# Operand splits of a gate/up product in pairs of 512 columns, in one fused attention and feed-forward kernel

## The chip, the cores and the metric

The kernel runs on one core of a Trainium2 chip. The metric is the device time of one launch in microseconds. Engine names are those of the profile: PE multiplies matrices (PEld is its weight load), DVE, ACT and POOL are the elementwise engines, SP issues the DMAs. Each takes its instructions in the order in which they were written.

## What is computed

One input x of 2048 rows by 576 columns goes through two branches, and a gate mixes them:

```python
g = sigmoid((x * gate_w).sum(-1, keepdims=True))
a = attention(x)                    # 32 heads of 18, four segments of 512, with a memory
b = (silu(x @ w_gate) * (x @ w_up)) @ w_down          # 576 -> 4608 -> 576
return g * a + (1 - g) * b
```

All of it is fp32. The change touches how the operands of `x @ w_gate` and `x @ w_up` are prepared.

## The kernel before, in words

**Splitting.** PE multiplies in a format that keeps fewer bits than fp32 (`fp32r` here). Each fp32 operand is therefore split in two: a *high* (ACT copies it into the fp32r tile) and a *remainder* (DVE subtracts the high from the source). A product then takes three multiplications: high by high, high by remainder of x, remainder by high of x. So every weight operand passes through ACT and DVE before PE can use it.

**Seven products.** The feed-forward's hidden columns are worked off in 36 slices of 128 (`FT`), for two halves of the rows: 72 *units*, `seq` in the code, numbered 0 to 71 below; half 0 is units 0 to 35. In a unit, gate and up weights form a 2 by 2 arrangement of blocks a11, a12, a21, a22 of 128 x 256 numbers each (x is arranged in the same way), and the four block products per result are made as seven, from sums of blocks. Operand 0 is a11, 1 is a21 + a22, 2 is operand 1 minus a11, 3 is a12, 4 is a11 - a21, 5 is a12 minus operand 2, 6 is a22. POOL makes the four sums. `seven(t, j)` issues the seven matrix instructions of operand j: for each of two blocks high, high, remainder (line 1027), then one for the rest of the rows (line 1030). A unit calls it for j = 0 to 6 in order, with elementwise work on ACT and DVE between: line 1096 after operand 2 (it waits for PE and for the copy of line 1092), 1103 and 1104 after operand 4, 1112 and 1113 after operand 6 (two multiplications on DVE that make the hidden values).

**Ticks.** After each of these pieces the unit calls `tick()`, eight times in all, numbered 0 to 7: tick j follows operand j for j up to 5, tick 6 follows tick 5 at once, tick 7 follows operand 6 and the multiplications. `tick` calls `beat`, which issues first what is *due* at this beat, then down-projection products (line 870) and attention steps. The work for a unit's weights is planned when the unit before it begins: `w_make` returns (number, function) pairs, and number n falls on the n-th beat from there, so 0 to 7 are the ticks of the unit before and 8 to 11 are ticks 0 to 3 of the unit that uses the weights. `HIGH[j]` and `LOW[j]` are the numbers of operand j's high (line 269) and remainder (line 272), `LEAD` places POOL's sums (line 265).

**Buffers.** Operands live in seven places of 2 KB a partition (`wop`); a high of the next unit may be written when the products that read the old one have run. POOL's sums go to three places of 1 KB (`ws`), raw weights to four of 2 KB (`raw`).

**Stages.** Every third unit carries the 16 down-projection groups of the three units before it and is long (about 35 us in the trace); the two others are short (12 to 13 us), with PE going from one operand to the next with at most an attention step between. In half 0 the down weights are split too (line 972, ACT and DVE) and stored; in half 1 they are fetched. The first two units' operands are stored to DRAM in half 0 (`keep`, line 275) and fetched in half 1 (`w_fetch`, line 713) in place of being made, numbers in `FIRST`. At the border of the halves, `x_second` loads, sums and splits the blocks of x for half 1; half of its raw blocks are put in operand places, numbers in `LOADS`, `SUMS`, `PARTS`. Ten further beats (`BREAK`) stand between the halves.

Of the kernel before, what the change touches and what calls it, by code (L numbers as in the profile page):

```python
# [20 lines left out]
P = 128  # L21
# [4 lines left out]
L = 512  # L26
# [17 lines left out]
QUIET = (5, 6, 7)  # L44
HELD = 4
LEAD = 3
HIGH = (2, 3, 3, 7, 7, 8, 9)
LOW = (5, 6, 7, 8, 9, 10, 11)
SHARE = (0, 0, 2, 2, 3, 3, 3, 3)
BREAK = 10  # L50
LOADS = ((-3, 0, 0), (-2, 0, 1), (3, 1, 0), (4, 1, 3), (4, 0, 3), (5, 0, 2), (5, 1, 1), (6, 1, 2))
SUMS = ((2, 0, 1), (9, 0, 4), (10, 1, 1), (11, 1, 4), (12, 1, 2), (13, 1, 6), (14, 0, 2), (19, 0, 6))
PARTS = ((1, 0, 0), (4, 0, 1), (10, 1, 0), (11, 1, 5), (12, 1, 3), (13, 0, 5), (13, 1, 1), (14, 1, 4), (15, 1, 2),
         (17, 0, 2), (17, 1, 6), (18, 0, 3), (20, 0, 4), (22, 0, 6))
FIRST = (9, 10, 11, 15, 17, 17, 19)
SLOT = (0, 3, 2, 1, 4, 6, 5)
RPOS = (0, 1, 4, 2, 5, 6, 3)
BLOCKS = {3: (4, 5), 6: (6, 7), 9: (8, 9), 12: (10, 11), 15: (12,), 18: (13,), 21: (14,), 24: (15,), 27: (16,), 30: (17,)}
# [3 lines left out]
def f32(ap):  # L62
    return ap.bitcast(F32)
# [3 lines left out]
def gated_mix(ctx, tc, xT, xrest, wf, wfr, wfh, wd, wv, wo, beta, cmask, ident, bmask, out):  # L67
# [3 lines left out]
    def pool(st, name, bufs, side="left", space=None):  # L71
        if space is None:
            return st.enter_context(tc.tile_pool(name=name, bufs=bufs, side=side))
        return st.enter_context(tc.tile_pool(name=name, bufs=bufs, space=space))
# [1 line left out]
    dram = pool(ctx, "dram", 1, space=bass.MemoryType.DRAM)  # L76
    stk = dram.tile([2, NSEG, D, 3, L], BF, name="stk")
    vd = dram.tile([NSEG, 2, P, 4, 16, 3, E], BF, name="vd")
    wc = dram.tile([KEPT, 7, P, 4 * P], F32, name="wc")
    rc = dram.tile([FT // 4, 96, 4, 7 * P], F32, name="rc")  # L80
    xrd = dram.tile([7, P, L], F32, name="xrd")
    dc = dram.tile([FT, P, 2 * D], F32, name="dc")
# [134 lines left out]
    def raw_tile():  # L217
        return rp.tile([P, L], F32, name="raw")
# [11 lines left out]

    wraw_of, wops, rhs = {}, {}, []

    def op_tile():
        return wop.tile([P, 2, 2, P], F32R, name="wo_")

    def r_block(h, o):
        i, c = divmod(h, 2)
# [16 lines left out]
    def r_fetch(f):  # L254
        nc.sync.dma_start(f32(rhs[f % 2][:96]).rearrange("p j n -> p (j n)"), rc[f // 4, :, f % 4])

    def w_make(half, f, LOW=LOW):
        g, u = wraw_of.pop(f)
        ops = wops[half, f] = [None] * 7
        a11, a12, a21, a22 = g[:, 0:2], g[:, 2:4], u[:, 0:2], u[:, 2:4]  # L260
        src = [a11, None, None, a12, None, None, a22]

        def total(j, p, q, sub=True):
            src[j] = rp.tile([P, 2, P], F32, name="ws", bufs=3)
            (nc.gpsimd.tensor_sub if sub else nc.gpsimd.tensor_add)(src[j], p(), q())  # L265

        def high(j):
            ops[j] = op_tile()
            nc.scalar.activation(ops[j][:, 0], src[j], AF.Copy)

        def low(j):
            nc.vector.tensor_sub(ops[j][:, 1], src[j], f32(ops[j][:, 0]))  # L272

        def keep(j):
            nc.sync.dma_start(wc[f, j], f32(ops[j]).rearrange("p a k n -> p (a k n)"))

        todo = [(LEAD - 2, lambda: total(1, lambda: a21, lambda: a22, False)),
                (LEAD - 1, lambda: total(2, lambda: src[1], lambda: a11)),
                (LEAD + 2, lambda: total(4, lambda: a11, lambda: a21)),
                (LEAD + 4, lambda: total(5, lambda: a12, lambda: src[2]))]  # L280
        for j in range(7):
            todo += [(HIGH[j], lambda j=j: high(j)), (LOW[j], lambda j=j: low(j))]
            if half == 0 and f < KEPT:
                todo.append((LEAD + j + 3, lambda j=j: keep(j)))
        return sorted(todo, key=lambda t: t[0])


# [1 line left out]
    with ExitStack() as st:  # L289
# [310 lines left out]
        for s in range(NSEG):  # L600
            upd = upd_gen(s - 1) if s else None
            casts = []
            for n, (m, u) in enumerate(chains):
                mid = []
                if s == 0:
                    for z in loads.get(n, []):
                        z()
                    if 0 < n < 6:
                        mid.append(lambda n=n: q_split(*chains[n + 3]))
                    if n in halves:  # L610
                        mid.append(lambda n=n: v_split(*halves[n]))
                if s == 1 and n < 3:
                    cast = masks(*((0, 3), (3, NT), (0, 0))[n])
                    casts.append(cast)
                if s == 1 and 3 <= n < 6:
                    mid.append(casts[n - 3])
                if (s, n) == (1, 7):
                    mid.append(betas)
                if (s, n) == (0, 3):
                    b_load(0)  # L620
                if (s, n) > (0, 3) and blocks:
                    mid.append(lambda z=blocks.pop(0): b_step(*z))
                if 1 <= s < 3:
                    if n == 2:
                        rest_load(2 - s)
                    for j in RSTEP.get(n, ()):
                        mid.append(lambda j=j: rest_split(2 - s, j) if j >= 0 else rest_sum(-j))
                if s == 3:
                    if 2 <= n < 6:
                        first_load(n - 2)  # L630
                    for j, z in FSUM.get(n, []):
                        mid.append(lambda j=j, z=z: first_sum(j, z))
                    for j, z in FSPLIT.get(n, []):
                        mid.append(lambda j=j, z=z: first_split(j, z))
                if s < 3:
                    for kt in ((0, 1), (2, 3), (4,))[n - 6] if s == 0 and n > 5 else (n - 4,) if s and n > 3 else ():
                        raws["x", kt] = x_load(s + 1, kt)
                qk(s, m, u, mid)
                flush(2)
                if upd is not None and n > 0:  # L640
                    next(upd, None)
            if s == 3:
                qst_.close()
                rp = pool(ctx, "rp", 4, side="right")
                wop = pool(ctx, "wop", 7, side="right")
                kq = pool(ast, "kq", 1, side="right")
                for i in range(NST):
                    qst.append(kq.tile([P, 2, L], BF, name=f"qst{i}"))
                    kst.append(kq.tile([P, 2, L], BF, name=f"kst{i}"))
                for i in range(2):  # L650
                    mbs.append(kq.tile([P, 8], F32, name=f"mb{i}"))
                for z in range(2):
                    for j, b, kt in ((0, 2, z), (3, 2, 2 + z), (5, 3, 2 + z)):
                        XO[j][z] = xs_of[b][0][kt]
                wraw_of[0] = [w_load(0, u) for u in range(2)]
                for z in range(2):
                    rhs.append(wop.tile([P, 7, P], F32R, name=f"rh{z}", bufs=1))
                start = w_make(0, 0, LOW[:3] + (7,) + LOW[4:])
            for n in range(8):
                hf, i = divmod(n, 4)  # L660
                flush()
                v_step(s, hf, i)
                if s and n % 2:
                    for bank in range(2):
                        mem_step(s, n // 2, bank)
                if s < 3:
                    if n == 0:
                        xs_of[s + 1] = x_tiles(s + 1)
                    if 1 <= n < 6:
                        x_split(xs_of[s + 1], n - 1, raws["x", n - 1])  # L670
                else:
                    if n == 4:
                        wraw_of[1] = [w_load(1, u) for u in range(2)]
                    if n < 2:
                        first_sum(6, n)
                    elif n < 6:
                        if n < 4:
                            nc.gpsimd.memset(f32(rhs[n - 2][96:]), 0.0)
                        if 3 <= n < 5:
                            r_fetch(n - 3)  # L680
                    if n > 2:
                        for z in stack_loads(0)[2 * n - 6:2 * n - 4]:
                            nc.sync.dma_start(*z)
                    for _ in range((0, 0, 2, 3, 3, 3, 3, 3)[n]):
                        if start[0][0] < 8:
                            start.pop(0)[1]()
# [5 lines left out]
    with ExitStack() as st:  # L692
# [15 lines left out]
        def w_fetch(f):  # L708
            ops = wops[1, f] = [None] * 7

            def one(j):
                ops[j] = op_tile()
                nc.sync.dma_start(f32(ops[j]).rearrange("p a k n -> p (a k n)"), wc[f, j])

            return [(j + 2 if f else FIRST[j], lambda j=j: one(j)) for j in range(7)]

        kp = pool(ast, "kp", 2, side="right")
        ap = pool(ast, "ap", 2, side="right")
# [273 lines left out]
            return [(f // CH, i, hf, hs, ds, yas[half], half) for i in range(8) for hf in range(2)]  # L992

        def x_second(new, rest):
            r = {}
            todo = []

            def load(z, q):
                b, kt = ((0, z), (1, z), (0, 2 + z), (1, 2 + z))[q]
                r[z, q] = wop.tile([P, L], F32, name="wo_") if z else raw_tile()[:, :L]  # L1000
                nc.sync.dma_start(r[z, q], xT[HALF[1][b], :, kt])

            def total(z, j):
# [224 lines left out]
```

## Time and profile before

| what | value |
|---|---|
| median of 3 runs | 1721.14 us (1719.92 to 1722.72) |
| the profiled execution | 1722.04 us, span of its instructions 1720.3 us |
| before the units, units of half 0, units of half 1, end | 221.57, 722.76, 683.67, 92.00 us |
| DMA | 328.05 MB, mean 191 GB/s |
| granted clock of PE | 1.00 |

How to read the rows of the next section: a row of the timeline has the start and the length in us, the engine, the line of the kernel, the operation, what it writes and reads, the shape and how many were merged; brackets tell how long the engine was idle before it and what it waited for. A row of busy time in stretches has the window, its length, then for each engine the busy time with the number of instructions in brackets, the granted clock, the DMAs' busy share and GB/s. A row of grouped instructions has count, then busy us and mean ns, then the idle time before them. Tiles named `wo__` with a number are operand places, each made by one call.

### The profile page before, as it was taken

How to read it: one execution, taken by the hardware profiler on the slowest of the kernel's cores; microseconds unless marked ns; L12 is line 12 of the kernel's file. 1: busy time of each engine (PE TensorE's matmuls, PEld its weight loads, DVE VectorE, ACT ScalarE, POOL GpSimd, SP SyncE). 2: the span in 40 equal slices, each digit the busy share in tenths (PEclk: the TensorE clock that was granted, in tenths of full speed). 3: DMA queues.
4: the chain of work that ended last, by engine and by line, in shares of the span. 5: the costliest groups of instructions: out<-in, count | busy, mean ns of one | idle time of the engine just before them, and what ended most of it. 6: DMA issues, size and time to landing. Idle time of an engine off the chain costs nothing.

```text
span 1720.3 us, 34819 instructions
## 1 busy us (share of the span) xinstructions
PE 1705.2 (99%) x11868; PEld 1479.8 (86%) x11868; DVE 1362.3 (79%) x3231; ACT 1084.6 (63%) x2123; POOL 937.9 (55%) x1194
## 2 busy tenths in 40 slices
PE   9999999999999999999999999999999999999999
PEld 7899978888888888888888788888888888888899
DVE  6557588888888889888889777787787788788655
ACT  7666576775776677567666756665666576566411
POOL 4434546666665655656566555565555555555311
PEclk9999999999999999999999999999999999999999
DMA  8654499998998898997979986787778677767633
GB/s 282 235 186 140 162 310 186 224 228 178 218 230 197 180 216 203 183 209 195 201 159 256 289 172 145 178 183 162 151 180 188 142 164 181 170 131 167 191 120 136
DMA packets 524002, 328.05 MB, mean 191 GB/s; under 512 B 411184, under 2 KB 460336, under 8 KB 523824
## 3 DMA queue, kind: packets, MB, share of 16 engines
q1 hardware_dynamic: 523824, 325.83, 78.0%
q8 instruction: 93, 1.52, 0.4%
q14 instruction: 85, 0.70, 0.1%
HBM read 165.76 MB, written 76.09 MB: 141 GB/s over the span
## 4 chain that ended last, share of the span: by engine, by line
PE 84%; DVE 7%; ACT 3%; issue 2%; DMA 2%; POOL 1%; SPq 0%; DVEq 0%; ACTq 0%; POOLq 0%
PE bank L1027 33%; PE bank L870 26%; PE bank L160 10%; PE bank L1030 5%; PE bank L728 4%; PE bank L776 2%; PE bank L777 1%; PE bank L415 1%; DVE hl L972 1%; DVE scr L734 1%; PE bank L461 1%; DVE dw L972 1%; DVE p L760 1%; PE bank L351 1%; DVE xo L138 1%
## 5 line engine op out<-in xcount | busy, mean ns | idle before, releaser
L761 POOL TENSOR_TENSOR p<-pe,p 128x512 f16<-128x512 f32 x320 | 378.4, 1182 | 417.0 <-DVE p L760 399.9
L870 PE MATMUL bank<-dw,hh 128*128 128x320 f32 (+1 forms) x2304 | 487.1, 304 | 1.5 <-DVE ya L880 1.5
L870 PEld LDWEIGHTS bank<-dw,hh 128*128 128x128 f32 x2304 | 381.1, 189 | 13.9 <-DVE ya L880 3.3
L746 ACT ACTIVATE pe<-bank,mb 128x512 f32<-128x512 f32 (+3 forms) x512 | 247.9, 526 | 196.2 <-DVE mb L734 183.1
L870 PE MATMUL bank<-dw,hl 128*128 128x320 f32 (+1 forms) x1152 | 340.6, 296 | 1.4 <-DVE hl L138 1.4
L734 DVE CUSTOM_DVE_ANT_0 scr<-bank,cm 128x512 bf16<-128x512 f32 (+3 forms) x512 | 246.5, 481 | 6.8 <-PE bank L728 0.2
L880 DVE TENSOR_TENSOR ya<-bank,ya 128x320 f32<-128x320 f32 x352 | 158.2, 453 | 77.8 <-PE bank L870 77.0
L870 PEld LDWEIGHTS bank<-dw,hl 128*128 128x128 f32 x1152 | 217.9, 189 | 1.9 <-DVE hl L138 1.9
L1030 PE MATMUL bank<-xr,rh 128*128 128x512 f32 x504 | 196.3, 390 | 0.0
L754 POOL TENSOR_SCALAR_AFFINE_SELECT pe<-pe 128x256 f32<-128x256 f32 (+1 forms) x320 | 151.6, 474 | 52.1 <-ACT pe L746 42.6
L760 DVE CAST p<-pe 128x512 f16<-128x512 f32 x320 | 160.6, 502 | 0.0
L265 POOL TENSOR_TENSOR ws<-raw 128x256 f32<-128x256 f32 x140 | 116.3, 831 | 16.1 <-DMA raw<-in_wf_dram 8.4
L728 PE MATMUL bank<-kst,qst 108*128 108x512 bf16 (+3 forms) x512 | 124.6, 305 | 0.3 <-DMA kst<-stk 0.2
L972 DVE TENSOR_TENSOR hl<-row,hh 128x512 fp32r<-128x512 f32 x120 | 108.4, 903 | 8.9 <-ACT hh L971 8.5
L1030 PEld LDWEIGHTS bank<-xr,rh 128*128 128x128 f32 x504 | 94.6, 188 | 20.4
L1104 DVE TENSOR_TENSOR row<-bank,row 128x512 f32<-128x512 f32 x72 | 49.7, 690 | 62.6 <-ACT bank L1103 62.5
L746 ACT ACT_TABLE_LOAD x69 | 88.5, 1283 | 10.8 <-DVE mb L734 9.8
L1089 ACT ACTIVATE bank<-bank 128x512 f32<-128x512 f32 x72 | 41.9, 582 | 79.8 <-PE bank L1030 76.7
L1106 ACT ACT_TABLE_LOAD x71 | 91.1, 1283 | 1.3
L1099 ACT ACTIVATE row<-bank 128x512 f32<-128x512 f32 x72 | 43.2, 600 | 71.5 <-PE bank L1030 71.3
L265 POOL TENSOR_TENSOR ws<-raw,ws 128x256 f32<-128x256 f32 x70 | 58.8, 840 | 49.9 <-DVE wo__22504 L272 9.7
L1103 ACT ACTIVATE bank<-bank 128x512 f32<-128x512 f32 x72 | 42.2, 587 | 65.5 <-PE bank L1030 65.1
(2170 smaller groups left out, 4123.1 us busy)
## 6 DMA issues: line engine op xcount, KB each, us to landing
raw<-in_wf_dram SPq DMA_DIRECT2D x140, 256.0 KB
rh<-rc SPq DMA_DIRECT2D x72, 336.0 KB
dc<-dw SPq DMA_DIRECT2D x36, 576.0 KB
dw<-dc SPq DMA_DIRECT2D x36, 576.0 KB
stk<-q SPq DMA_DIRECT2D x32, 384.0 KB
draw<-in_wd_dram SPq DMA_DIRECT2D x36, 288.0 KB
rc<-rt SPq DMA_DIRECT2D x42, 224.0 KB
vd<-vps SPq DMA_DIRECT2D x8, 912.0 KB
```

What stands on the lines that cost most here:

```text
L160: nc.tensor.matmul(t, st[n], mv[n], start=(n == 0), stop=(n == 13))
L265: (nc.gpsimd.tensor_sub if sub else nc.gpsimd.tensor_add)(src[j], p(), q())
L728: nc.tensor.matmul(t[:, c:c + w], qs[:KR, pr, P * i:P * i + P], ks[:KR, pr, 0:w], start=True, stop=True)
L734: nc.vector.tensor_tensor_reduce(scr[:, :w], t[:, c:c + w], cm[:, L - w:L], -SCALE, 3.0e38, OP.add, OP.min, m[:, k:k + 1])
L746: nc.scalar.activation(pe[:, c:c + w], t[:, c:c + w], AF.Exp, bias=m[:, k:k + 1], scale=SCALE)
L754: nc.gpsimd.affine_select(d, d, pattern=pat, compare_op=OP.is_ge, fill=0.0, base=0, channel_multiplier=1)
L760: nc.vector.tensor_copy(p[:, 0], pe)
L761: nc.gpsimd.tensor_sub(p[:, 1], pe, p[:, 0])
L870: nc.tensor.matmul(ts[m], p, q[:, cs], start=(n == 0), stop=(n == 3 * CH - 1))
L880: nc.vector.tensor_add(ya[:, i, cs], t, ya[:, i, cs])
L1027: nc.tensor.matmul(t, w[:, p, z], x[z][:, q], start=first and n == 0, stop=False, skip_group_check=True)
L1030: nc.tensor.matmul(t, rem[:, RPOS[j]], XR[j], start=False, stop=True, skip_group_check=True)
```

## The change

Operands are made in pairs, `PAIRS = ((0, 3), (1, 2), (4, 6), (5,))`. A pair shares one place of 4 KB (operand 5 keeps one of 2 KB), one high of 512 columns on ACT and one remainder of 512 columns on DVE; so a unit has four highs and four remainders in place of seven and seven. To make that possible the sources lie side by side: operands 0 and 3 are the raw gate block, 1 and 2 are two halves of one `ws` place of 2 KB, and operand 4's sum is written over a21, so that 4 and 6 are the raw up block; operand 5's sum has a place of its own (`wt`). Each place exists once. The numbers are rewritten: pair by pair, highs on 4, 3, 8, 9 and remainders on 6, 7, 10, 11. Stores and fetches of kept operands move a whole place at a time, and the raw x blocks that lay in operand places lie in `ws`, in operand 5's place and in the place of operands 4 and 6, with other numbers in `LOADS`.

```diff
-HIGH = (2, 3, 3, 7, 7, 8, 9)
-LOW = (5, 6, 7, 8, 9, 10, 11)
+PAIRS = ((0, 3), (1, 2), (4, 6), (5,))
+HIGH = (4, 3, 8, 9)
+LOW = (6, 7, 10, 11)
-LOADS = ((-3, 0, 0), (-2, 0, 1), (3, 1, 0), (4, 1, 3), (4, 0, 3), (5, 0, 2), (5, 1, 1), (6, 1, 2))
+LOADS = ((-3, 0, 0), (-2, 0, 1), (2, 1, 0), (4, 0, 3), (5, 0, 2), (6, 1, 1), (8, 1, 3), (8, 1, 2))
-FIRST = (9, 10, 11, 15, 17, 17, 19)
+FIRST = ((9, 10, 18, 15), (4, 3, 8, 6))
...
-    def op_tile():
-        return wop.tile([P, 2, 2, P], F32R, name="wo_")
+    def op_tile(g, shape=None, dtype=F32R):
+        n = len(PAIRS[g])
+        return wop.tile(shape or [P, 2, n, 2, P], dtype, name=f"wo{'abcd'[g]}_", bufs=1)
+
+    def op_home(f, g):
+        return wc[f, :, 8 * P * g:8 * P * g + 4 * P * len(PAIRS[g])]
+
+    def op_views(ops, g, t):
+        for i, j in enumerate(PAIRS[g]):
+            ops[j] = t[:, :, i]
...
-        src = [a11, None, None, a12, None, None, a22]
+        part = {4: a21}
+        src = {0: g, 2: u}
+        tile_of = {}
         def total(j, p, q, sub=True):
-            src[j] = rp.tile([P, 2, P], F32, name="ws", bufs=3)
-            (nc.gpsimd.tensor_sub if sub else nc.gpsimd.tensor_add)(src[j], p(), q())
+            if j == 1:
+                src[1] = rp.tile([P, 4, P], F32, name="ws", bufs=1)
+                part[1], part[2] = src[1][:, 0:2], src[1][:, 2:4]
+            elif j == 5:
+                part[5] = src[3] = rp.tile([P, 2, P], F32, name="wt", bufs=1)
+            (nc.gpsimd.tensor_sub if sub else nc.gpsimd.tensor_add)(part[j], p(), q())
-        def high(j):
-            ops[j] = op_tile()
-            nc.scalar.activation(ops[j][:, 0], src[j], AF.Copy)
-        def low(j):
-            nc.vector.tensor_sub(ops[j][:, 1], src[j], f32(ops[j][:, 0]))
+        def high(n):
+            tile_of[n] = op_tile(n)
+            op_views(ops, n, tile_of[n])
+            nc.scalar.activation(halves(n, 0), flat(n), AF.Copy)
+        def low(n):
+            nc.vector.tensor_sub(halves(n, 1), flat(n), f32(halves(n, 0)))
...
-        for j in range(7):
-            todo += [(HIGH[j], lambda j=j: high(j)), (LOW[j], lambda j=j: low(j))]
+        for n in range(4):
+            todo += [(HIGH[n], lambda n=n: high(n)), (LOW[n], lambda n=n: low(n))]
             if half == 0 and f < KEPT:
-                todo.append((LEAD + j + 3, lambda j=j: keep(j)))
+                todo.append((LOW[n] + 1, lambda n=n: keep(n)))
...
-                start = w_make(0, 0, LOW[:3] + (7,) + LOW[4:])
+                start = w_make(0, 0)
...
-            return [(j + 2 if f else FIRST[j], lambda j=j: one(j)) for j in range(7)]
+            return [(FIRST[f][n], lambda n=n: one(n)) for n in range(4)]
...
-                r[z, q] = wop.tile([P, L], F32, name="wo_") if z else raw_tile()[:, :L]
+                if not z:
+                    r[z, q] = raw_tile()
+                elif q == 0:
+                    r[z, q] = rp.tile([P, L], F32, name="ws", bufs=1)
+                elif q == 1:
+                    r[z, q] = op_tile(3, [P, L], F32)
+                else:
+                    if not pair:
+                        pair.append(op_tile(2, [P, 2, L], F32))
+                    r[z, q] = pair[0][:, q - 2]
```

More of the change, by code (lines that the diff above doesn't have):

```diff
@@ L78, in gated_mix @@
     vd = dram.tile([NSEG, 2, P, 4, 16, 3, E], BF, name="vd")
-    wc = dram.tile([KEPT, 7, P, 4 * P], F32, name="wc")
+    wc = dram.tile([KEPT, P, 28 * P], F32, name="wc")
     rc = dram.tile([FT // 4, 96, 4, 7 * P], F32, name="rc")
@@ L231, in gated_mix, with op_flat @@
     wraw_of, wops, rhs = {}, {}, []
-    def op_tile():
-        return wop.tile([P, 2, 2, P], F32R, name="wo_")
+    def op_tile(g, shape=None, dtype=F32R):
+        n = len(PAIRS[g])
+        return wop.tile(shape or [P, 2, n, 2, P], dtype, name=f"wo{'abcd'[g]}_", bufs=1)
+    def op_flat(t):
+        return f32(t).rearrange("p a j k n -> p (a j k n)")
+    def op_home(f, g):
[3 more added lines that the diff above has]
+            ops[j] = t[:, :, i]
     def r_block(h, o):
@@ L255, in r_fetch, with w_make @@
         nc.sync.dma_start(f32(rhs[f % 2][:96]).rearrange("p j n -> p (j n)"), rc[f // 4, :, f % 4])
-    def w_make(half, f, LOW=LOW):
+    def w_make(half, f):
         g, u = wraw_of.pop(f)
@@ L271, in low @@
-        def low(j):
-            nc.vector.tensor_sub(ops[j][:, 1], src[j], f32(ops[j][:, 0]))
-        def keep(j):
-            nc.sync.dma_start(wc[f, j], f32(ops[j]).rearrange("p a k n -> p (a k n)"))
+            if j == 1:
[4 more added lines that the diff above has]
+            (nc.gpsimd.tensor_sub if sub else nc.gpsimd.tensor_add)(part[j], p(), q())
@@ new lines, in flat, with halves, keep @@
+        def flat(n):
+            return src[n].rearrange("p k n -> p (k n)")
+        def halves(n, z):
+            return tile_of[n][:, z].rearrange("p j k n -> p (j k n)")
+        def high(n):
[4 more added lines that the diff above has]
+            nc.vector.tensor_sub(halves(n, 1), flat(n), f32(halves(n, 0)))
+        def keep(n):
+            nc.sync.dma_start(op_home(f, n), op_flat(tile_of[n]))
@@ L277, in w_make @@
         todo = [(LEAD - 2, lambda: total(1, lambda: a21, lambda: a22, False)),
-                (LEAD - 1, lambda: total(2, lambda: src[1], lambda: a11)),
+                (LEAD - 1, lambda: total(2, lambda: part[1], lambda: a11)),
                 (LEAD + 2, lambda: total(4, lambda: a11, lambda: a21)),
-                (LEAD + 4, lambda: total(5, lambda: a12, lambda: src[2]))]
-        for j in range(7):
-            todo += [(HIGH[j], lambda j=j: high(j)), (LOW[j], lambda j=j: low(j))]
+                (LEAD + 4, lambda: total(5, lambda: a12, lambda: part[2]))]
@@ L644, in gated_mix @@
                 rp = pool(ctx, "rp", 4, side="right")
-                wop = pool(ctx, "wop", 7, side="right")
+                wop = pool(ctx, "wop", 1, side="right")
                 kq = pool(ast, "kq", 1, side="right")
@@ L709, in w_fetch, with one @@
             ops = wops[1, f] = [None] * 7
-            def one(j):
-                ops[j] = op_tile()
-                nc.sync.dma_start(f32(ops[j]).rearrange("p a k n -> p (a k n)"), wc[f, j])
-            return [(j + 2 if f else FIRST[j], lambda j=j: one(j)) for j in range(7)]
+            def one(n):
+                t = op_tile(n)
+                op_views(ops, n, t)
+                nc.sync.dma_start(op_flat(t), op_home(f, n))
+            return [(FIRST[f][n], lambda n=n: one(n)) for n in range(4)]
         kp = pool(ast, "kp", 2, side="right")
@@ L994, in x_second @@
         def x_second(new, rest):
-            r = {}
+            r, pair = {}, []
             todo = []
```

## The prediction, made before the result

> **What bounds the kernel now.** I read the page first, then the busy time in stretches, then the waits, then the timeline of single units. On the page:
>
> ```profile
> span 1720.3 us, 34819 instructions
> PE 1705.2 (99%) x11868; PEld 1479.8 (86%) x11868; DVE 1362.3 (79%) x3231; ACT 1084.6 (63%) x2123; POOL 937.9 (55%) x1194
> PE 84%; DVE 7%; ACT 3%; issue 2%; DMA 2%; POOL 1%; SPq 0%; DVEq 0%; ACTq 0%; POOLq 0%
> PE bank L1027 33%; PE bank L870 26%; PE bank L160 10%; PE bank L1030 5%; PE bank L728 4%; PE bank L776 2%; PE bank L777 1%; PE bank L415 1%; DVE hl L972 1%; DVE scr L734 1%; PE bank L461 1%; DVE dw L972 1%; DVE p L760 1%; PE bank L351 1%; DVE xo L138 1%
> ```
>
> PE is busy 99% and carries 84% of the chain that ended last; the products of this change's operands (L1027) are a third of it. The span is 1720.3 us; that execution took 1722.04 us, 0.9 above the median of 1721.14, and my sum is added to the median. Cut by stage (before the units, units of half 0, units of half 1, the end), columns PE, PEld, DVE, ACT, POOL:
>
> ```profile
> 221.57:944.33 722.76, 715.72 (x5094) 610.26 (x5092) 634.36 (x1504) 491.34 (x950) 443.64 (x580) 1.00 0.92 210
> 944.33:1628.00 683.67, 682.77 (x4830) 588.23 (x4829) 537.88 (x1311) 435.73 (x843) 371.17 (x471) 1.00 0.76 174
> ```
>
> In the 72 units PE is idle 722.76 - 715.72 = 7.0 us in half 0 and 0.9 us in half 1, at a granted clock of 1.00. So whatever is taken off another engine can return about 8 us here, no more. The reader should keep this asymmetry: little to win, and any new wait of PE costs its full length. DVE is the second engine (634 of 723 us in half 0), and works in order.
>
> **What the change removes.** The highs (L269, ACT) and remainders (L272, DVE) of the operands, over both halves:
>
> ```profile
> 214.00:944.00 730.00, 146.10 (x252) 1.00 0.92 210
> 944.00:1628.00 684.00, 135.96 (x238) 1.00 0.76 174
> 214.00:944.00 730.00, 98.95 (x252) 1.00 0.92 210
> 944.00:1628.00 684.00, 92.58 (x238) 1.00 0.76 174
> L971 ACT ACTIVATE hh<-row 128x512 fp32r<-128x512 f32 x120 | 75.3, 628 | 0.9 <-DVE row L1113 0.9
> L972 DVE TENSOR_TENSOR hl<-row,hh 128x512 fp32r<-128x512 f32 x120 | 108.4, 903 | 8.9 <-ACT hh L971 8.5
> L138 DVE TENSOR_TENSOR hl<-row,hh 128x512 fp32r<-128x512 f32 x24 | 17.8, 743 | 11.3 <-ACT hh L137 11.0
> ```
>
> The first two rows are L272 (DVE), the next two L269 (ACT), 490 = 70 units x 7 each. A remainder costs (146.10 + 135.96) / 490 = 0.58 us on average, a high 191.5 / 490 = 0.39. Three remainders of 512 columns at 0.74 to 0.90 and one of 256 at 0.58 are 2.8 to 3.3 us, against 4.0 for seven: DVE is relieved by 0.7 to 1.2 us a unit. Three highs at 0.63 and one at 0.39 are 2.3, against 2.7: ACT by 0.4. All of this lies beside PE.
>
> [...]
>
> **What the change moves.** This decides. The operands of a unit are read one after the other, 7 products each; highs are read by products 1, 2, 4, 5, remainders from the third on. A pair is written whole, so it can only be written after both old operands are read, and must be there before the earlier of the two is read. With the tick numbers of HIGH and LOW (8 ticks a unit, number 8 is the next unit's tick 0):
>
> - Operand 0's remainder moves from tick 5 to 6, where operand 1's was; the unit reads it first.
> - Operand 1's moves from tick 6 to 7, where operand 2's was: behind the two multiplications L1112 and L1113, the first of which waits for the last operand of the old unit. It is read second.
> - Operand 4's moves from tick 1 to 2, behind L1096. Operand 5's moves from tick 2 to 3, where operand 6's was.
>
> So each new deadline can be tested in the old trace: put the remainder that stood at the later place beside the products that will now need it. Operand 1, in a unit without down-products:
>
> ```profile
> 1264.20 1.00 DVE L272 TENSOR_TENSOR wo__17859<-raw,wo__17859 128x256 fp32r<-128x256 f32 x1
> 1265.13 0.51 DVE L272 TENSOR_TENSOR wo__17872<-ws,wo__17872 128x256 fp32r<-128x256 f32 x1
> 1265.22 1.52 PE L1027 MATMUL bank<-xo,wo__17859 128*128 128x512 f32 x6
> 1265.56 0.68 DVE L1112 TENSOR_TENSOR row<-bank,row 128x512 f32<-128x512 f32 x1
> 1266.16 0.68 DVE L1113 TENSOR_TENSOR row<-row 128x512 f32<-128x512 f32 x1
> 1266.76 0.95 DVE L272 TENSOR_TENSOR wo__17874<-ws,wo__17874 128x256 fp32r<-128x256 f32 x1
> 1266.80 1.52 PE L1027 MATMUL bank<-xo,wo__17872 128*128 128x512 f32 x6
> ```
>
> Seven products take 1266.80 - 1265.22 = 1.58 us, 0.226 each, so the third product of operand 1 starts at 1266.80 + 0.45 = 1267.25. The remainder at the later place ends at 1266.76 + 0.95 = 1267.71: 0.46 us too late, and it will be twice as wide. The same for operand 0 (first three rows) and operand 5 (last three):
>
> ```profile
> 499.96 1.72 DVE L972 TENSOR_TENSOR dw<-draw,dw 128x576 fp32r<-128x576 f32 x1
> 500.52 1.52 PE L1027 MATMUL bank<-xo,wo__6605 128*128 128x512 f32 x6
> 501.60 0.62 DVE L272 TENSOR_TENSOR wo__6635<-ws,wo__6635 128x256 fp32r<-128x256 f32 x1
> ...
> 976.02 0.41 DVE L272 TENSOR_TENSOR wo__13668<-ws,wo__13668 128x256 fp32r<-128x256 f32 x1
> 978.28 1.64 PE L1027 MATMUL bank<-xo,wo__13668 128*128 128x512 f32 x6
> 978.64 0.80 DVE L272 TENSOR_TENSOR wo__13702<-raw,wo__13702 128x256 fp32r<-128x256 f32 x1
> ```
>
> Operand 0 is needed at 500.97, the later place ends at 502.22: 1.25 late, because DVE still splits a down weight. Operand 5 is needed at 978.73, the later place ends at 979.44: about 0.6 to 0.7 late. I took this difference for all 70 units (first and last of them here):
>
> ```profile
> 221.57 1.62 PE L1027 MATMUL bank<-xo,wo__2469 128*128 128x512 f32 x6
> 221.71 0.42 DVE L272 TENSOR_TENSOR wo__2471<-ws,wo__2471 128x256 fp32r<-128x256 f32 x1
> ...
> 1617.64 1.66 PE L1027 MATMUL bank<-xo,wo__22833 128*128 128x512 f32 x6
> 1618.96 0.45 DVE L272 TENSOR_TENSOR wo__22835<-ws,wo__22835 128x256 fp32r<-128x256 f32 x1
> ```
>
> The later place ends after the need in 18 units for operand 0, 20 for operand 1, 1 for operand 4 and 16 for operand 5; 39 units have at least one. A stall of PE also delays the reads behind it, so a unit counts its largest shortfall only: the sum is **25.5 us**, 18.9 of it in half 0.
>
> Two things shift that sum. The wider remainder ends later by 256 columns, 0.69 - 0.42 = 0.27 us alone (L1112 and wo__2471 bracket it); with 0.27 on every unit the sum is 37. Against it DVE has fewer operations ahead, which helps only where it was behind and not where it waited for PE (L1112 and L1096 do, in most short units); 0.27 earlier in every unit gives 16, 0.5 earlier 10. I take them as cancelling, since about half the late units wait at L1112 or L1096 just before. The waits that exist today can shrink:
>
> ```profile
> PEld bank L1027 <- ACT bank L1103: 6.3, 10, 1.3
> PEld bank L1027 <- DVE bank L1096: 5.0, 9, 1.1
> ```
>
> I take off 2 us of these 11, as ACT's and DVE's order around L1103 and L1096 hardly changes.
>
> **The other edits.** Stores of kept operands (units 0 and 1 alone) become four of up to 512 KB. Today's:
>
> ```profile
> 227.75 5.12 DMA wc<-wo__2473
> 232.96 0.42 ACT L269 ACTIVATE wo__2722<-ws 128x256 fp32r<-128x256 f32 x1 [2.25 <-DMA wc<-wo__2473]
> ```
>
> 256 KB took 5.12 us and held ACT 2.25 us, three ticks behind. Twice the bytes at the same distance holds ACT longer, at most by another 5 us a store; PE sees part. I take 2 us, from 0 to 10, for both units. At the border of the halves the raw x blocks are loaded into the new homes up to four ticks later, and the third fetch comes at tick 0 of the unit that reads it at its fifth operand, some 7 us later, against 5.12 for half the bytes in the row above. I take 1 us, from -1 to 5. Fewer DMA issues on SP cost nothing: PE waits for none of them. The sums on POOL stay at four of the same size, and their waits for a free buffer get shorter, off the chain.
>
> Sum: 25.5 - 2 + 2 + 1 = 26.5, so 1721.1 + 26.5 = **1748 us**.
>
> **The rivals.**
>
> 1. *Relief before deadline (faster).* DVE's 0.7 to 1.2 us a unit come in ahead of the late places. For: in half 0 DVE is 88% busy, and where it runs behind PE everything later moves forward. If it gains more than the shortfall in nearly all units (the largest is 1.7), no new wait stays and at most 8 us of today's idle goes: about 1714. The point is a relief of about 1 us before tick 6; against it, two of the three remainders removed (operands 3 and 4, ticks 0 and 1) lie behind these ticks, and L1112 waits for PE whatever DVE has saved. [...]
> 2. *New waits and relief meet* within 3 us of now: 1721. It needs 1 us of relief at the late places, which leaves under 4 us of shortfall.
> 3. *Wider remainders meet POOL.* The late places already show 0.80 and 0.95 where 0.41 is the time alone; if the wide ones take 0.9 to 1.2 there, shortfalls grow by about 0.45 without relief: 47 us, 1768. [...]
> 4. *The edit does less than it says*: the shortfalls are absorbed, and only the two stores and the border count: about 1726.
>
> **How the numbers follow.** Forecast 0.66; rivals 0.12, 0.05, 0.10 and 0.07 in order. A measurement here tells about 0.2% (3.4 us) from nothing. Faster 0.12 is rival 1; within 0.2% is 0.05; slower is 0.66 + 0.10 + 0.07 = 0.83. The range runs from 1722, which leaves out rival 1 and half of rival 2, to 1768: the forecast's own terms span 10 to 47 us, and rival 4 lies inside.
>
> **What would show it.** PE idle in front of L1027, released by DVE L272, in units without down-products, at the third product of the first, second and sixth operands, 20 to 45 us in all, more in half 0. Today's sum of such waits is one row under L272 (us, times):
>
> ```profile
>   PEld bank L1027: 1.9, 6
> ```
>
> DVE's busy time for L272 down by 50 to 80 us, ACT's for L269 by about 30, with PE's idle up all the same. The forecast is wrong if L272 releases PE for under 10 us, if the lost time lies at the border of the halves, or if L1096 or L1103 become the releasers.

## The result and the profile after

The changed kernel takes **1761.19 us** (median of 5 runs, 1760.46 to 1762.06) against 1721.14: a ratio of 1.0229, 95% interval [1.0218, 1.0241]. That is 40 us more. The profiled execution took 1762.06 us with a span of 1760.0. The forecast was 1748 us, with a range from 1722 to 1768.

In the new kernel lines have moved: the high is L294 (L269 before), the remainder L297 (L272), POOL's sums L283, a unit's products L1062 and L1065, and L1092, L1096, L1103, L1106, L1112 and L1113 are now L1127, L1131, L1138, L1141, L1147 and L1148. The page:

```profile
span 1760.0 us, 34418 instructions
PE 1720.0 (98%) x11868; PEld 1473.7 (84%) x11868; DVE 1310.4 (74%) x3021; ACT 1064.1 (60%) x1913; POOL 939.2 (53%) x1194
PE 63%; ACT 7%; DVE 6%; issue 5%; POOL 3%; DMA 2%; SPq 1%; DVEq 0%; ACTq 0%; POOLq 0%
```

DVE has 51.9 us less to do and ACT 20.5, and the kernel is slower. PE's share of the chain fell from 84% to 63%, but the shares add up to 87% of the span here and to 99% before, so the chain alone doesn't tell how much PE lost. The stages, cut where the units begin, change halves and end:

```profile
222.71:966.72 744.01, 723.74 (x5094) 607.42 (x5092) 607.30 (x1396) 480.21 (x843) 444.04 (x579) 1.00 0.89 204
966.72:1669.60 702.88, 690.11 (x4830) 585.34 (x4829) 514.58 (x1209) 426.18 (x741) 373.52 (x474) 1.00 0.73 170
```

Half 0 is 21.3 us longer and half 1 19.2, at the same clock and with the same number of PE instructions. PE's idle time went from 7.0 to 20.3 us and from 0.9 to 12.8. Its *busy* time also rose, by 8.0 and 7.3 us: where products follow one another, only 0.23 us of each counts; the last one ahead of a wait counts with its full 0.39 (the two products ahead of the wait shown below count 0.61). So idle time alone shows too little of a wait. Who waits for the remainders (us, times; the PE row was missing before, the PEld row stood at 1.9, 6):

```profile
  PEld bank L1062: 55.6, 85
  PE bank L1062: 24.2, 42
  POOL ws L283: 5.2, 4
  POOL wt L283: 2.6, 2
```

One such wait, in a short unit of half 1, at operand 1:

```profile
1292.67 0.58 ACT L1138 ACTIVATE bank<-bank 128x512 f32<-128x512 f32 x1 [0.53 <-PE bank L1065]
1293.16 0.62 ACT L294 ACTIVATE woa__17301<-raw 128x512 fp32r<-128x512 f32 x1
1293.69 0.68 ACT L772 ACTIVATE pe<-bank,mb 128x512 f32<-128x512 f32 x1
1294.39 1.28 ACT L1141 ACT_TABLE_LOAD   x1
1294.39 1.17 POOL L787 TENSOR_TENSOR p<-pe,p 128x512 f16<-128x512 f32 x1 [4.62 <-DVE p L786]
1294.84 1.27 DVE L297 TENSOR_TENSOR woa__17301<-raw,woa__17301 128x512 fp32r<-128x512 f32 x1
...
1295.68 0.63 ACT L1141 ACTIVATE row<-row 128x512 f32<-128x512 f32 x1
...
1296.23 0.74 POOL L283 TENSOR_TENSOR raw<-raw 128x256 f32<-128x256 f32 x1
1296.35 0.69 DVE L1147 TENSOR_TENSOR row<-bank,row 128x512 f32<-128x512 f32 x1 [0.24 <-ACT row L1141]
1296.93 0.73 POOL L283 TENSOR_TENSOR wt<-raw,ws 128x256 f32<-128x256 f32 x1
1296.95 1.26 DVE L1148 TENSOR_TENSOR row<-row 128x512 f32<-128x512 f32 x1
1297.45 0.61 PE L1062 MATMUL bank<-xo,wob__17289 128*128 128x512 f32 x2
1298.14 0.68 DVE L297 TENSOR_TENSOR wob__17289<-ws,wob__17289 128x512 fp32r<-128x512 f32 x1
1298.87 1.20 PE L1062 MATMUL bank<-xo,wob__17289 128*128 128x512 f32 x4 [0.81 <-DVE wob__17289 L297]
```

Operand 1's third product is due at 1297.45 + 0.45 = 1297.90. Its remainder (`wob__17289`, last but one row) stands behind the two multiplications, as the prediction put it, ends at 1298.82, and PE goes on at 1298.87, 0.97 us late. Two more things can be read here. The first multiplication (L1147) waits for ACT: the wide high L294 at tick 4 stands between ACT's copy L1138 and its activation L1141. And two of DVE's operations are longer where POOL works: the wide remainder takes 1.27 us beside POOL's and 0.68 beside none, and the second multiplication 1.26 beside POOL's, against 0.68 on average in the 35 units in which POOL does nothing beside it.

To put a price on each place, I set the start of every operand's first and third product beside the same product of the kernel before. The difference is the lag; what it grows by between two such points is lost between them. At third products: operand 0 lost 6.8 us, operand 1 15.3, operand 5 11.0, in 45 units. Another 8.6 us appear at the first products of operands 1, 2 and 6, most of it as 0.11 or so behind each wait: the product behind one that waited starts 0.34 us after it instead of 0.23, so a wait costs more than its length here. The old waits at operand 4 shrink by 2.8 in half 0, and 1.1 is lost ahead of the first unit. Followed back on DVE, the last wait ahead of a late remainder is at L1147 for 25 of the 27 of operand 1 (19 times for ACT's L1141) and at L1131 for 16 of the 17 of operand 5: the instructions behind which the new numbers put them.

### The profile page after: what moved, and what is told of

Same layout as the page of the kernel before. It is cut to its first block, busy times and chain, and to the rows that moved or that the text cites. A ratio compares the mean times of both kernels' runs of the same rounds, so it can differ in the third digit from the quotient of the medians.

```text
span 1760.0 us, 34418 instructions
## 1 busy us (share of the span) xinstructions
PE 1720.0 (98%) x11868; PEld 1473.7 (84%) x11868; DVE 1310.4 (74%) x3021; ACT 1064.1 (60%) x1913; POOL 939.2 (53%) x1194
## 4 chain that ended last, share of the span: by engine, by line
PE 63%; ACT 7%; DVE 6%; issue 5%; POOL 3%; DMA 2%; SPq 1%; DVEq 0%; ACTq 0%; POOLq 0%
PE bank L896 24%; PE bank L1062 24%; PE bank L1065 4%; PE bank L161 3%; PE bank L754 3%; PE bank L802 2%; ACT L1141 1%; PE bank L803 1%; ACT pe L772 1%; POOL ws L283 1%; ACT bank L1138 1%; ACT row L1141 1%; POOL p L787 1%; DVE p L786 1%; DVE hl L998 1%
## 5 line engine op out<-in xcount | busy, mean ns | idle before, releaser
L1065 PE MATMUL bank<-xr,rh 128*128 128x512 f32 x504 | 196.6, 390 | 0.0
L786 DVE CAST p<-pe 128x512 f16<-128x512 f32 x320 | 156.6, 491 | 0.0
L1065 PEld LDWEIGHTS bank<-xr,rh 128*128 128x128 f32 x504 | 94.6, 188 | 20.8
L1139 DVE TENSOR_TENSOR row<-bank,row 128x512 f32<-128x512 f32 x72 | 49.7, 690 | 63.3 <-ACT bank L1138 63.0
L1138 ACT ACTIVATE bank<-bank 128x512 f32<-128x512 f32 x72 | 42.1, 584 | 71.6 <-PE bank L1065 71.5
L1131 DVE TENSOR_TENSOR bank<-bank,row 128x512 f32<-128x512 f32 x72 | 50.3, 699 | 46.2 <-PE bank L1065 25.3
L1147 DVE TENSOR_TENSOR row<-bank,row 128x512 f32<-128x512 f32 x72 | 49.8, 691 | 46.3 <-PE bank L1065 27.0
```

Of the source, the lines that this page charges most:

```text
L786: nc.vector.tensor_copy(p[:, 0], pe)
L1065: nc.tensor.matmul(t, rem[:, RPOS[j]], XR[j], start=False, stop=True, skip_group_check=True)
```

## The experiments

**The theory** was that the places (tick numbers) of the remainders make the loss, and that DVE's relief buys nothing. **The rivals**: the wide operation (its length, POOL beside it, both operands of a pair at once); ACT's order; stores, fetches and the border. The kernel before took 1720.5 to 1721.7 us beside these runs (medians); differences under about 3.4 us, the prediction's measure, are not told from nothing by the times alone. Where operands are named with a number of us, it is the loss at their third products.

**1. All remainders one tick earlier.**

```diff
-LOW = (6, 7, 10, 11)
+LOW = (5, 6, 9, 10)
```

> The changed kernel with its four remainders one tick earlier (numbers 5, 6, 9, 10 for 6, 7, 10, 11); pairs, places and widths stay. Theory 'place': PE waits because the tick puts the remainder behind work that itself waits for PE (L1112 and L1113 above all), so nearly all of the 33 us gained at the third products of operands 0, 1 and 5 goes: 1718 to 1730 us. Rival 'width': an operation of 512 columns is what is late, as it collides with POOL and runs 0.7 to 0.9 us wherever it stands: over 1745. Rival 'homes': stores, fetches and raw x blocks in new homes carry the loss: 1755 to 1761.

Measured: 1728.94 us (1727.84 to 1730.62), ratio 1.0053 [1.0038, 1.0068]. The waits are gone (rows as above):

```profile
  PEld bank L1062: 2.6, 7
  POOL wt L283: 1.6, 1
  PE bank L1062: 0.2, 1
```

32 of the 40 us go with the place alone; pairs, width, stores and border are all still there, and hold at most 8.

**2. The kernel before, with the late numbers.** Seven highs and seven remainders of 256 columns, moved to where the change has them.

```diff
-HIGH = (2, 3, 3, 7, 7, 8, 9)
-LOW = (5, 6, 7, 8, 9, 10, 11)
+HIGH = (4, 3, 3, 4, 8, 9, 8)
+LOW = (6, 7, 7, 6, 10, 11, 10)
```

> The kernel before, seven single highs and remainders in seven places of 2 KB, with only their numbers set to those of the changed kernel (highs 4, 3, 3, 4, 8, 9, 8; remainders 6, 7, 7, 6, 10, 11, 10). 'Place': it loses what the changed kernel lost or more, since DVE has three more operations to do at the same places: 1755 to 1775 us. 'Width' and 'homes': no change from before, 1719 to 1727.

Measured: 1751.83 us (1751.38 to 1752.38), ratio 1.0186 [1.0171, 1.0201], a little under what was expected. The late places, of highs and remainders together, cost 31 us without any pair. Rows of those who wait for L272:

```profile
  POOL ws L265: 179.8, 82
  PEld bank L1027: 45.6, 67
  PE bank L1027: 21.0, 33
  POOL pe L754: 1.0, 3
```

Operands 0, 1 and 5 lose 3.8, 5.2 and 18.7 us. POOL waits 179.8 us for its `ws` places; of the waits that the late remainders stand behind on DVE, none was ended by POOL. ACT's order is in these 31 us too, since the highs of operands 0 and 3 also moved, from ticks 2 and 7 to tick 4: ahead of the first multiplication DVE waits 19.1 us for ACT's L1106, where it waited 3.6 before.

```profile
L1112 DVE TENSOR_TENSOR row<-bank,row 128x512 f32<-128x512 f32 x72 | 49.6, 690 | 36.7 <-ACT row L1106 19.1 <-PE bank L1030 15.0 <-ACT dw L971 1.8
```

**3 to 6. One or two remainders one tick earlier.** The changed kernel, with the first, second, sixth, or first and second number of `LOW` put back by one:

```diff
-LOW = (6, 7, 10, 11)
+LOW = (6, 6, 10, 11)    # operands 1 and 2
+LOW = (6, 7, 10, 10)    # operand 5
+LOW = (5, 7, 10, 11)    # operands 0 and 3
+LOW = (5, 6, 10, 11)    # operands 0 to 3
```

Operands 1 and 2:

> The changed kernel with the remainder of operands 1 and 2 alone one tick earlier (6 for 7), ahead of the two multiplications. 'Place': the third products of operand 1, where 15.3 us were gained on the trace before, no longer wait, with about 3 us that follow each wait: 1761 - 18 = 1743, 1738 to 1750. 'Width' or 'homes': 1757 to 1763.

Operand 5:

> The changed kernel with the remainder of operand 5 alone one tick earlier (10 for 11); this one is 256 columns wide as before. 'Place': the third products of operand 5, where 11.0 us were gained, no longer wait, with some 2 us that follow: 1761 - 13 = 1748, 1744 to 1754. 'Width': operation of 256 columns, so what it costs now is not width; if width elsewhere is the cause, its shift changes nothing, 1757 to 1763.

Operands 0 and 3:

> The changed kernel with one number of LOW moved, 6 to 5: the remainder of operands 0 and 3 is issued one tick earlier, everything else stays. In the changed kernel PE loses 6.8 us at the third product of operand 0 and 15.3 us at that of operand 1. If the waits at the deadlines were independent of one another, the 6.8 us and the 1 us or so of refilling behind them would go: 1753 us. If a wait taken away comes back at the next deadline (as it did where operand 5's remainder alone was moved), operand 1's third product, which follows 1.6 us later with the same DVE queue before it, takes up most of it: over 20 us there, and 1756 to 1761 us.

Operands 0 to 3:

> The changed kernel with two numbers of LOW moved, 6 to 5 and 7 to 6: the remainders of operands 0 and 3 and of operands 1 and 2 one tick earlier, those of 4, 6 and 5 as in the changed kernel. Independent waits: the 6.8 and 15.3 us at the first two operands go, with some 3 us of refilling, the 11 us at operand 5 stay: 1735 to 1737 us. If the waits move on to the next deadline, operand 5's third product rises above 14 us and the time is 1739 to 1743 us. In either case the kernel with all remainders one tick earlier, 1729 us, tells what operand 5 alone is worth when the others are in time: 7 us by the first, 10 to 14 by the second, where it was worth 3 when the others were late.

| remainders moved | op. 0 | op. 1 | op. 5 | us (lowest to highest) | ratio and interval |
|---|---|---|---|---|---|
| none (the change) | 6.8 | 15.3 | 11.0 | 1761.19 (1760.46 to 1762.06) | 1.0229 [1.0218, 1.0241] |
| 0 and 3 | 0 | 19.8 | 10.7 | 1759.58 (1756.66 to 1760.46) | 1.0215 [1.0197, 1.0234] |
| 5 | 12.0 | 17.8 | 0 | 1758.13 (1756.97 to 1758.33) | 1.0221 [1.0206, 1.0236] |
| 1 and 2 | 6.9 | 0 | 12.0 | 1742.56 (1742.41 to 1745.54) | 1.0137 [1.0121, 1.0154] |
| 0 to 3 | 0 | 0.3 | 11.7 | 1737.24 (1735.00 to 1739.37) | 1.0091 [1.0073, 1.0109] |

The expectation for operands 1 and 2 held. That for operand 5 failed: the time lies in the range that was given to 'width', but the waits at operand 5 did go and came back elsewhere, which neither reading said. Of the two readings given for the others, the moving wait held for operands 0 and 3, and 0 to 3 together came closest to independence. Operand 1 is worth its price (18.6 us); operands 0 and 5 return 1.6 and 3.1, neither clear of the noise and not the 7 to 12 that PE loses at them. Their waits go, but reappear at the deadlines behind: for operand 5 moved, those who wait for L297 are

```profile
  PEld bank L1062: 47.6, 65
  PE bank L1062: 24.0, 39
```

so PE's own idle for remainders is as before (24.2), on fewer operands. I read it so, and no run tests it alone: a wait of PE lets DVE catch up, and without it DVE meets the next deadline further behind. With operands 0 to 3 in time, operand 5's step is worth 1737.24 - 1728.94 = 8.3 us (with operands 4 and 6, which move too). So a place has no fixed price: operand 5's tick is worth at most some 3 us or about 8, depending on the others.

**7. Pair highs, seven remainders of 256 columns** on the numbers of before:

```diff
+LOWS = (5, 6, 7, 8, 9, 10, 11)
-            todo += [(HIGH[n], lambda n=n: high(n)), (LOW[n], lambda n=n: low(n))]
+            todo += [(HIGH[n], lambda n=n: high(n))]
+            for i, j in enumerate(PAIRS[n]):
+                todo += [(LOWS[j], lambda n=n, i=i: low(n, i))]
```

> The changed kernel with its four highs and places, but seven remainders of 256 columns at the numbers of the kernel before (5, 6, 7, 8, 9, 10, 11). 'Place': the waits for remainders go whatever the highs and homes are: 1722 to 1730 us, about where the kernel with four remainders one tick earlier landed (1728.9). If it lands under that by over 3 us, the width of the remainders cost something there; if above by over 3, their number did. 'Homes': 1752 or more.

Measured: 1727.24 us (1725.34 to 1729.19), ratio 1.0036 [1.0022, 1.0049], as 'place' expected. The four wide remainders of run 1, on time, are no better than seven narrow ones: fewer, wider operations gain PE nothing here.

**8. Highs earlier too**, on top of run 1.

```diff
-HIGH = (4, 3, 8, 9)
+HIGH = (4, 3, 7, 8)
-LOW = (6, 7, 10, 11)
+LOW = (5, 6, 9, 10)
```

> The changed kernel with remainders at 5, 6, 9, 10 and the last two highs one tick earlier too (4, 3, 7, 8). With the remainders moved, 3.4 us of the rest were gained at the first product of operand 4, which waits for L1131, which waits for ACT's copy, behind the high of operands 4 and 6 at tick 0. 'ACT's order carries the rest': 1728.9 - 3 = 1726, 1723 to 1727. 'The border and the homes carry the rest': 1727.5 to 1730, no change.

Measured: 1727.80 us (1725.92 to 1730.28), ratio 1.0040 [1.0028, 1.0053]: not told apart from run 1.

**9. Earlier still.** As run 8, with `LOW = (5, 4, 8, 9)`.

> Highs at 4, 3, 7, 8 and remainders each as early as its place and its high allow: 5, 4, 8, 9. 'Place': each remainder has two ticks or more before its first reader, no wait for one is left: 1720 to 1727, at or under the kernel with 5, 6, 9, 10. 'Too early does harm, as the remainder of operands 4 and 6 then stands ahead of the hidden values' remainders (L998)': 1727 to 1735.

Measured: 1733.61 us (1732.66 to 1734.35), ratio 1.0073 [1.0059, 1.0086], slower than run 8. Operand 0 loses 9.2 us again, in 26 units, although its own number is unchanged. In 25 of them the wide remainder of operands 1 and 2, now at tick 4, stands on DVE between L1139, where DVE last waited, and operand 0's remainder. So it was early that did harm, but by another remainder than the expectation named. This is read from the trace; no run tried it alone.

**10. The change's places, each pair's remainder as two operations of 256 columns** at the same tick.

```diff
-            nc.vector.tensor_sub(halves(n, 1), flat(n), f32(halves(n, 0)))
+            for i in range(len(PAIRS[n])):
+                c = slice(2 * P * i, 2 * P * i + 2 * P)
+                nc.vector.tensor_sub(halves(n, 1)[:, c], flat(n)[:, c], f32(halves(n, 0)[:, c]))
```

> The changed kernel, numbers included, with each remainder of a pair issued as two operations of 256 columns, one behind the other. 'Width': operations of 512 columns carry the 9 us between the changed kernel (1761) and the singles at its numbers (1752): back to 1750 to 1755. 'Homes, stores and ACT carry the 9 us': 1760 to 1766, the halves costing the same or a little more. 'Place' alone decides nothing between these two.

Measured: 1755.39 us (1754.86 to 1756.29), ratio 1.0200 [1.0186, 1.0213], 5.8 below the change and just above the range given to 'width'. DVE has more to do:

```profile
PE 1718.2 (98%) x11868; PEld 1475.8 (84%) x11868; DVE 1341.2 (76%) x3231; ACT 1063.9 (61%) x1913; POOL 923.8 (53%) x1194
```

DVE works 1341.2 - 1310.4 = 30.8 us more and the kernel is faster. I put that down to the operand read first, which is released after half the pair: operand 0 falls from 6.8 to 4.5 and operand 1 from 15.3 to 8.7, while operand 5, which has no pair, rises from 11.0 to 16.2.

**11. The high of operands 0 and 3 at tick 3**, off the stretch of ACT between L1138 and L1141.

```diff
-HIGH = (4, 3, 8, 9)
+HIGH = (3, 3, 8, 9)
```

> The changed kernel with one number of HIGH moved, 4 to 3: the high of operands 0 and 3 stands one tick earlier on ACT, ahead of the copy after operand 4 and no longer between that copy and the activations behind it; the remainders stay where the change puts them. In the changed kernel DVE stands 14.5 us, in 20 units, in front of the first multiplication for ACT's first activation, where it stood 3.6 us in 6 units before; operand 1's remainder is the second instruction behind that multiplication. Theory that a part of operand 1's waits comes by way of ACT: DVE's 14.5 falls to about 4, operand 1's third product loses 10 us at most and 5 to 8 likely, 1751 to 1756 us. Theory that the number of the remainder alone decides: the multiplication waits for PE just as long, operand 1's 15.3 us stay, 1758 to 1762 us.

Measured: 1754.62 us (1753.59 to 1757.18), ratio 1.0197 [1.0183, 1.0212]. The first multiplication on DVE, in groups with what ended the idle time ahead of it, in the kernel before, the changed one, and this one:

```profile
L1112 DVE TENSOR_TENSOR row<-bank,row 128x512 f32<-128x512 f32 x72 | 49.6, 689 | 31.6 <-PE bank L1030 25.3 <-ACT row L1106 3.6 <-ACT wo__11024 L269 1.6
```
```profile
L1147 DVE TENSOR_TENSOR row<-bank,row 128x512 f32<-128x512 f32 x72 | 49.8, 691 | 46.3 <-PE bank L1065 27.0 <-ACT row L1141 14.5 <-ACT row L1143 4.0
```
```profile
L1147 DVE TENSOR_TENSOR row<-bank,row 128x512 f32<-128x512 f32 x72 | 49.7, 690 | 37.2 <-PE bank L1065 33.8 <-ACT row L1141 2.2 <-ACT dw L997 0.8
```

DVE's wait for ACT falls from 14.5 to 2.2 us, operand 1 from 15.3 to 9.4, the time by 6.6. So ACT's late high is a second way by which the change makes operand 1 late. It overlaps with run 10's 5.8 (both act on operand 1); they were not run together.

**12. The same number in the kernel of run 7.**

> The kernel with highs in pairs and seven remainders of 256 columns at the numbers of before (1727 us, of which the kernel before needs 1721) with the same number of HIGH moved, 4 to 3. DVE stands 9.0 us for ACT in front of the first multiplication in it, but hardly any product waits for a remainder. If the wait is off PE's path there: 1725 to 1729 us, no change. If the rest of some 6 us over the kernel before comes by way of ACT's order: 1720 to 1724 us, and no slower than the kernel before.

Measured: 1729.00 us (1726.26 to 1731.39), ratio 1.0039 [1.0025, 1.0053]: no change, so the rest of 6 to 8 us isn't this part of ACT's order; run 8, which moved the last two highs, gained nothing clear either. In its trace, 3.6 us of the 9.3 lost in the span stand at one product, the first of operand 4 in the first unit of half 1, which waits for its fetch:

```profile
PE bank L1066 <- DMA woc__13070<-wc: 3.4, 1, 3.4
```

In run 1 this wait is 0.4 us, and 1.3 at the next unit's first operand. In the changed kernel as it is, PE is later and doesn't wait for this fetch; at the next unit's first operand PEld's row for the fetch has 0.9 us, and PE loses 0.6. This is the border that the prediction priced at -1 to 5. The rest is spread over some first products of operands 1, 4 and 6 and the first two units, and stays open. No version was faster than the kernel before.

## Why the prediction was right, and where its size was off

**What bounds, and what can be gained.** Right. DVE's busy time for remainders fell from 282.1 to 217.6 us and ACT's for highs from 191.5 to 160.2, within the 50 to 80 and about 30 forecast, and PE got none of it.

**The places.** Right in mechanism and in which operands, and in the total of the places. Read from the old trace, 39 units should be late (18, 20, 1 and 16 times at operands 0, 1, 4 and 5), by 25.5 us with the largest of each unit. In run 2, where only the places changed, 40 units are late, by 26.7 us counted in the same way (18.0 in half 0). In the changed kernel it is 45 units (12, 27, 1 and 17 times) and 30.5 us: 17.5 in half 0 (18.9 forecast), but 13.0 in half 1 (6.6). How close the totals are is in part luck: operand by operand the old trace gives 12.2, 14.4 and 8.0 us at operands 0, 1 and 5, where run 2 lost 3.8, 5.2 and 18.7 and the change 6.8, 15.3 and 11.0. Run 2 also holds ACT's later high, which the 25.5 left out.

**"I take them as cancelling"** (the wider remainder against DVE's relief). This step failed in size, by 30.5 - 25.5 = 5.0 us. Run 10 puts the width at 5.8 us, and run 1 beside run 7 finds no use of the relief. The growth lies in half 1, where at operand 1, 15 of 34 units had had only 0 to 0.6 us of slack; with the remainders in halves (run 10) half 1's 13.0 falls to 10.1. The prediction also left out ACT: the wide high between L1138 and L1141 (run 11, 6.6 us, partly the same microseconds). It had priced the highs by their sum, which falls, and not by their new tick.

**"A unit counts its largest shortfall only."** Also too low, and by more. With all waits of a unit it is 34 us at third products instead of 30.5, since a second wait in one unit still costs. And a new wait of PE did not cost "its full length" but more: the 8.6 us behind the waits were not in the sum at all, the largest single part of what the forecast missed.

**The small terms.** The old waits shrank by 2.8 us (2 forecast). Stores of kept operands (2 forecast): units 0 and 1 lost 0.9 us together, waits for remainders included. The border (1 forecast) cost about 0.6 in the changed kernel's trace and 1.7 to 3.6 in versions where PE is on time.

**The rivals.** *Relief before deadline* is refuted by runs 1, 7 and 10: one remainder of 512 columns does take less of DVE than two of 256 (0.68 us above, against 0.42 for each of 256 in `wo__2471`'s row of the trace before, POOL at rest beside both), but saving that was worth less than having half the pair earlier. *Wider remainders meet POOL* has a true part, 1.27 us beside POOL and 0.68 alone in the rows above; over the changed kernel's trace a wide remainder takes 0.93 us on average in the 121 cases with POOL at work beside it and 0.68 in the 89 without. Not every operation of DVE is longer there: L1147, which reads a bank, takes 0.69 us in the 50 units with POOL beside it and in the 22 without, and L1148, which reads none, 1.05 in 37 and 0.68 in 35. But the rival's price of 20 us more than the forecast was too high; the result lies between the two. *Meet within 3 us* and *the edit does less* fell with the result; the latter's 5 us for stores and border is near the 6 to 8 that stay when the places are put right, of which the border is shown for 1.7 to 3.6 and the rest is open.

## What to carry to other kernels

Where operations move on an in-order engine, compare each new place with the start of its first reader in the old trace, unit by unit: that gave 25.5 us here where a run of the places alone gave 26.7, in total though not by operand. Then count every wait, add what follows each (0.11 us here), and do the same for the engine that feeds the moved one, ACT's tick as well as DVE's. Merging two operations makes the first reader wait for both: issuing them apart again at the same tick returned 5.8 us (run 10), and the 51.9 us that the change took off DVE, which wasn't the bound, did not pay for that.

## What the runs showed of the hardware that was not expected

In the changed kernel's trace a wait in the middle of an operand's products cost PE about 0.11 us more than its length: the product behind it followed after 0.34 us instead of 0.23. And waits of PE didn't add up: 11.0 us of them taken away at operand 5 returned at most some 3 us, with 7.7 us more at operands 0 and 1.
